# Attention scores of the split pairs: three half-row fp32r passes for two heads at once, in place of two full-row passes for each head

## The chip, the cores and the metric

The kernel runs on one core of a Trainium2 chip. The metric is the device time of one execution in microseconds (us), the median of several runs. A profiled execution gives the trace that the text reads.

## What is computed

Sigmoid attention over 8 batches, 12 heads, 448 rows and 64 columns for a head, and then a bilinear feed-forward network on the 3584 tokens:

```python
scores = scale * np.matmul(q, k.transpose(0, 1, 3, 2)) - np.log(S)
attn = 1.0 / (1.0 + np.exp(-scores))
x = np.matmul(attn, v).transpose(0, 2, 1, 3).reshape(B * S, H * D)
out = (((x @ w1) * (x @ w2)) @ w3) @ w_out
```

Everything is float32. The weights come as 64-bit words that the kernel decodes itself.

## The kernel before

**Pairs and chunks.** Two heads make a pair, since 2 x 64 columns fill 128 partitions; there are 48 pairs. The 448 rows of k are cut into four chunks: three of 128 rows and a short one of 64. For a pair, the kernel goes through the chunks in the order 0, short, 1, 2 (`chunks`); each is one slot of the program. In a slot stand a chunk's scores on TensorE (PE), its sigmoid on ScalarE (ACT), then twelve matmuls of the network's first layer (`take(filler, ups)`, line 361, tile `up`), and then the products with v that are due (`attend`, tile `av`).

**Plain and split pairs.** The first 13 pairs (`PLAIN`) use float32 operands as they are; there, the two heads of a pair stand in the lower and upper 64 partitions, and each head's scores are a matmul over 64 rows (line 200). In the trace such a float32 matmul is two records. The other 35 pairs are split: an operand is written as a rounded high part and the remainder as a low part, both fp32r, whose matmul is one record. The `up` matmuls start with the second slot of the first split pair, so from there on each slot holds work for TensorE that depends on nothing in the slot.

**Scores of a split pair before.** q and k are loaded twice, so that both halves of the partitions hold the same 64 rows. `split_pair` makes `qs` (the high part in the lower 64 partitions, the low part in the upper ones), `kh` and `kl` (high and low part of k in both halves). A matmul of `kh` with `qs` over all 128 rows then sums high and low part of q in one pass, and a second one with `kl` adds the rest: two passes for each head, four for a chunk (line 203). For the short chunk, `ks` holds the high and low parts of its 64 rows of k side by side as 128 columns; one pass for each head (line 229) gives two halves, which `add_halves` (lines 190 and 191) adds with two copies on ACT and two additions on VectorE (DVE). `short_attention` then needs three activations and two subtractions (line 243). A split pair has 3 x 4 + 2 = 14 score passes.

**After the scores.** `attention` runs the sigmoid twice, once into fp32r (`ah`) and once in place (`sp`); DVE subtracts the one from the other (line 221, `al`). The scores stand in PSUM, in two buffers of the tile `sp`. Two more PSUM tiles hold the `av` sums, two the `up` sums.

**Order.** PE and SP (the queue that issues the DMAs) run in the order in which the code is written. For the split pairs, a scheduler sets the order on ACT, DVE and POOL (GpSimd).

The part of the program that this is about, the loop over the pairs, stands at the end of the function printed here.

Of the kernel before, what the change touches and what calls it, by code (L numbers as in the profile page):

```python
# [11 lines left out]
F32 = mybir.dt.float32  # L12
F32R = mybir.dt.float32r
U32 = mybir.dt.uint32
AF = mybir.ActivationFunctionType
ALU = mybir.AluOpType
# [9 lines left out]
def sigmoid_attention_bilinear_ffn(  # L26
# [16 lines left out]
    nc = tc.nc  # L43
    B, H, D, S = qT.shape
    DM, DF = w1.shape[0], w1.shape[1] // 2
    NT = B * S
    P = 128
    CHUNKS = [(c, min(P, S - c)) for c in range(0, S, P)]
    NC = len(CHUNKS)
    assert 2 * D == P and CHUNKS[-1][1] == D  # L50
    NPAIR = H // 2
# [10 lines left out]
    PLAIN = 2 * NPAIR + 1  # L62
# [3 lines left out]
    ps = phase_s.enter_context(tc.tile_pool(name="ps", bufs=3, space=PSUM))  # L66
# [5 lines left out]
    def split(dst_hi, dst_lo, src, hi_engine, lo_engine):  # L72
        hi_engine(out=dst_hi, in_=src)  # L73
        lo_engine.tensor_tensor(out=dst_lo, in0=src, in1=dst_hi, op=ALU.subtract)  # L74
# [40 lines left out]
    pa = phase_a.enter_context(tc.tile_pool(name="pa", bufs=2, side="right"))  # L115
# [10 lines left out]
    def load_pair(b, hp):  # L126

        heads = slice(2 * hp, 2 * hp + 2)
        if b * NPAIR + hp < PLAIN:

            qk = pa.tile([P, 2, S], F32, name="qp", tag="qk", bufs=3)
            for i, src in enumerate((qT, kT)):
                nc.sync.dma_start(out=qk[:, i], in_=src[b, heads].rearrange("h d s -> (h d) s"))
            return qk[:, 0], qk[:, 1]
        qq = pa.tile([P, 2, S], F32, name="qq", tag="qk", bufs=3)
        kk = pa.tile([P, 2, S], F32, name="kk", tag="qk", bufs=3)
        for dst, src in ((qq, qT), (kk, kT)):
            for r in range(2):
                nc.sync.dma_start(
                    out=dst[r * D:(r + 1) * D], in_=src[b, heads].rearrange("h d s -> d h s")  # L140
                )
        return qq, kk

    def load_v(b, hp):
        vv = pa.tile([P, NC, 2 * D], F32, name="vv")
# [6 lines left out]
            nc.sync.dma_start(out=vv[r * D:(r + 1) * D, NC - 1], in_=v[b, full:, cols])  # L152
        return vv

    def split_pair(plain, qq, kk):

        if plain:
            return qq, kk, None, None
        qs = pf[0].tile([P, 2, S], F32R, name="qs")
        kh = pf[0].tile([P, 2, S], F32R, name="kh")  # L160
        kl = pf[0].tile([P, 2, S], F32R, name="kl")
        nc.vector.tensor_copy(out=qs, in_=qq)
        nc.vector.tensor_tensor(out=qs[D:], in0=qq[D:], in1=qs[D:], op=ALU.subtract)
        split(kh, kl, kk, nc.vector.tensor_copy, nc.gpsimd)

        ks = pf[0].tile([P, 2, P], F32R, name="ks")
        for j in range(2):
            for i, k in ((j, kh), (1 - j, kl)):
                nc.gpsimd.tensor_copy(out=ks[:, j, i * D:(i + 1) * D], in_=k[:, j, S - D:])
        return qs, kh, kl, ks  # L170

    def split_v(plain, vv):
        if plain:
            return vv

        vs = pf[0].tile([P, NC, 2, 2, D], F32R, name="vs")
        for j in range(2):
            split(vs[:, :, j, j, :], vs[:, :, j, 1 - j, :], vv[:, :, j * D:(j + 1) * D],
                  nc.vector.tensor_copy, nc.gpsimd)
        return vs  # L180

    def sigmoid(dst, src):
        n = src.shape[0]
        nc.scalar.activation(dst, src, AF.Sigmoid, bias=bias[:n], scale=scale)  # L184

    def add_halves(dst, src):

        for j in range(2):
            rows, others = slice(j * D, (j + 1) * D), slice((1 - j) * D, (2 - j) * D)
            nc.scalar.copy(out=dst[rows], in_=src[j][others])  # L190
            nc.vector.tensor_tensor(out=dst[rows], in0=src[j][rows], in1=dst[rows], op=ALU.add)

    def scores(qs, kh, kl, c):

        at, n = CHUNKS[c]
        sp = ps.tile([P, 2, 512], F32, name="sp", bufs=2)[:n, :, :S]
        for j in range(2):
            if kl is None:
                rows = slice(j * D, (j + 1) * D)
                nc.tensor.matmul(sp[:, j], kh[rows, at:at + n], qs[rows], start=True, stop=True)  # L200
                continue
            for m, k in enumerate((kh, kl)):
                nc.tensor.matmul(sp[:, j], k[:, j, at:at + n], qs[:, j], start=m == 0, stop=m == 1)  # L203
        return sp

    def attention(plain, sp):

        n = sp.shape[0]
        if plain:
            a = pa.tile([P, 2, S], F32, name="ap", tag="ah", bufs=3)[:n]  # L210
            sigmoid(a, sp)
            return (a,)
        ah = pa.tile([P, 2, S], F32R, name="ah", tag="ah", bufs=3)
        sigmoid(ah[:n], sp)
        sigmoid(sp, sp)
        if n < P:

            nc.vector.tensor_tensor(out=ah[n:], in0=sp, in1=ah[:n], op=ALU.subtract)
            return (ah,)
        al = pf[0].tile([P, 2, S], F32R, name="al")  # L220
        nc.vector.tensor_tensor(out=al, in0=sp, in1=ah, op=ALU.subtract)  # L221
        return ah, al

    def short_scores(ks, qs):


        sp = ps.tile([P, 2, 512], F32, name="sp", bufs=2)[:, :, :S]
        for j in range(2):
            nc.tensor.matmul(sp[:, j], ks[:, j], qs[:, j], start=True, stop=True)  # L229
        t = pa.tile([P, S], F32, name="st", tag="t")  # L230
        add_halves(t, [sp[:, j] for j in range(2)])
        return t

    def short_attention(t):

        a = pa.tile([P, 2, S], F32R, name="ah", tag="ah", bufs=3)
        for j in range(2):
            rows = slice(j * D, (j + 1) * D)
            sigmoid(a[rows, j], t[rows])
        sigmoid(t, t)  # L240
        for j in range(2):
            rows, others = slice(j * D, (j + 1) * D), slice((1 - j) * D, (2 - j) * D)
            nc.vector.tensor_tensor(out=a[others, j], in0=t[rows], in1=a[rows, j], op=ALU.subtract)  # L243
        return (a,)

    def attend(c, ops, v, accs):

# [140 lines left out]
    pairs = [(b, hp) for b in range(B) for hp in range(NPAIR)]  # L388
# [11 lines left out]
    qks, vvs = {}, {}  # L400
# [8 lines left out]
    warm = ps.tile([P, 512], F32, name="up", tag="up", bufs=2)  # L409
    for _ in range(16):  # L410
        nc.tensor.matmul(warm[:, :S], zeros[:, :P], zeros, start=True, stop=True)
    splits, vs = {0: split_pair(0 < PLAIN, *qks.pop(0))}, {0: split_v(0 < PLAIN, vvs.pop(0))}
    first = decode_first()
    take(first, 1)
    xs = {n: [] for n in range(NU)}
# [2 lines left out]
    waiting = []  # L418
    accs = {}
    pf = []  # L420
# [14 lines left out]
    def prepare(p, i):  # L435

        n = p + 1
        change = n in (PLAIN, PLAIN + 1)
        if i == (2 if change else 1) and n < len(pairs):
            splits[n] = split_pair(n < PLAIN, *qks.pop(n))  # L440
        if i == 0 and change:
            qks[n] = load_pair(*pairs[n])
        if i == 1 and n < len(pairs):
            vvs[n] = load_v(*pairs[n])
        if i == NC - 1 and n < len(pairs):
            vs[n] = split_v(n < PLAIN, vvs.pop(n))
        n = p + 2
        if i == (0 if n < PLAIN else 2) and n not in (PLAIN, PLAIN + 1) and n < len(pairs):
            qks[n] = load_pair(*pairs[n])

    def x_due(slot):
        for at in [k for k in xts if (k[0] * NPAIR + k[1] + 1) * NC < slot]:
# [9 lines left out]
    chunks = [0, NC - 1, *range(1, NC - 1)]  # L464
    ups = NF * 2 * NK * 3 // PER
    slot = 0
    for p, (b, hp) in enumerate(pairs):
        if p == PLAIN - 1:
            order.close()
            order.enter_context(tc.manual_schedule(engines={ET.PE, ET.SP}))  # L470
        plain = p < PLAIN
        qs, kh, kl, ks = splits.pop(p)
        for i, c in enumerate(chunks):
            if (p, i) == (PLAIN - 1, 2):
                phase_p.close()
                pf.append(phase_a.enter_context(tc.tile_pool(name="pf", bufs=2, side="right")))
            prepare(p, i)
            if not plain and i == 1:
                short = short_scores(ks, qs)
            else:  # L480
                sp = scores(qs, kh, kl, c)
                if not plain and i == 2:
                    waiting.append((slot + 1, p, NC - 1, short_attention(short)))
                waiting.append((slot + 1, p, c, attention(plain, sp)))
            if slot == 0:
                take(first, 10)
            for at, j, stage in steps:
                if at == slot:
                    decode_weights(j, stage)
            x_due(slot)  # L490
            if slot >= BEGIN:
                take(filler, ups)
            attend_due(slot)
            slot += 1
# [25 lines left out]
    for jc in range(NF):  # L520
        take(filler, 10)
        for half in range(2):
            ms = slice(half * NM, (half + 1) * NM)
            src = w_out[jc * P:(jc + 1) * P].rearrange("p (m u) -> p m u", u=2)[:, ms]
# [110 lines left out]
    for i, ic in enumerate(ics):  # L635
        c, second = divmod(i, 2)
# [4 lines left out]
        for half in range(2):  # L641
            ms = slice(half * NM, (half + 1) * NM)
            acc = ps2.tile([P, 512], F32, name="up", tag="acc", bufs=8)
            for jc in range(NF):
                for m, (a, w) in enumerate(((w3h, woh), (w3h, wol), (w3l, woh))):
                    nc.tensor.matmul(  # L646
                        acc[:, :NM], a[:, jc], w[:, jc, ms],
                        start=(jc == 0 and m == 0), stop=(jc == NF - 1 and m == 2),
                    )
            nc.scalar.copy(out=stage[:, 2 * second + half], in_=acc[:, :NM])  # L650
            name = ("b11", None, "b21", "b22")[2 * second + half]
# [109 lines left out]
```

## Time and profile before

| | us |
|---|---|
| median of 3 runs | 1058.15 (1057.02 to 1058.85) |
| the profiled execution, its own time | 1057.37 |
| its span | 1055.5 |
| PE busy | 1042.1 |
| weight loads of PE (PEld) busy | 847.1 |
| DVE busy | 793.8 |
| ACT busy | 592.6 |
| POOL busy | 164.2 |

The stage of the plain pairs lasts to about 110 us, the split pairs to about 700 us, and the layers after them to the end. PE and PEld are one engine: a matmul and the load of its stationary operand, which can run under the matmul before it. A matmul's record holds its passage through the array too, so records overlap; the distance from one start to the next is the time that a pass takes. In a row such as `64*128` after the word MATMUL, the first number is the rows and the second the columns of the array that the matmul uses; `128*128` is the whole array. The chain is the list of work that ended last, followed back from the end.

### The profile page before, as it was taken

How to read it: one execution, taken by the hardware profiler on the slowest of the kernel's cores; microseconds unless marked ns; L12 is line 12 of the kernel's file. 1: busy time of each engine (PE TensorE's matmuls, PEld its weight loads, DVE VectorE, ACT ScalarE, POOL GpSimd, SP SyncE). 2: the span in 40 equal slices, each digit the busy share in tenths (PEclk: the TensorE clock that was granted, in tenths of full speed). 3: DMA queues.
4: the chain of work that ended last, by engine and by line, in shares of the span. 5: the costliest groups of instructions: out<-in, count | busy, mean ns of one | idle time of the engine just before them, and what ended most of it. 6: DMA issues, size and time to landing. Idle time of an engine off the chain costs nothing.

```text
span 1055.5 us, 14196 instructions
## 1 busy us (share of the span) xinstructions
PE 1042.1 (99%) x4820; PEld 847.1 (80%) x4820; DVE 793.8 (75%) x1248; ACT 592.6 (56%) x877; POOL 164.2 (16%) x249
## 2 busy tenths in 40 slices
PE   9998999999999999999999999999999999999998
PEld 3222688888888888888888888878899999999997
DVE  6998788877787787787878777668826677868572
ACT  6887676676667667676666766653324443324230
POOL 0000423222232322223231322100000000000000
PEclk9999999999999999999999999999999999999999
DMA  9886664555546454554555545144324555657542
GB/s 283 261 282 192 157 175 122 164 150 141 137 124 179 133 156 130 142 166 125 137 143 156 154 129 146 41 158 135 115 93 147 181 186 194 223 174 227 174 141 79
DMA packets 118983, 167.56 MB, mean 159 GB/s; under 512 B 10176, under 2 KB 96128, under 8 KB 118912
## 3 DMA queue, kind: packets, MB, share of 16 engines
q1 hardware_dynamic: 118912, 166.67, 52.7%
q8 instruction: 38, 0.62, 0.3%
q14 instruction: 33, 0.27, 0.1%
HBM read 125.73 MB, written 40.89 MB: 158 GB/s over the span
## 4 chain that ended last, share of the span: by engine, by line
PE 91%; DMA 4%; DVE 3%; ACT 1%; issue 1%; SPq 1%; ACTq 0%; DVEq 0%
PE up L361 41%; PE up L679 20%; PE av L259 9%; PE sp L203 8%; PE up L646 5%; PE sp L200 4%; PE av L252 3%; PE sp L229 1%; DMA raw<-w3T 1%; DMA x_dram<-t 1%; DMA vv<-vL 1%; ACT ap L184 1%; DMA graw<-g_dram 0%; DMA qq<-qT 0%; DVE w3l L74 0%
## 5 line engine op out<-in xcount | busy, mean ns | idle before, releaser
L361 PE MATMUL up<-xh,w 128*128 128x512 f32 x1344 | 438.9, 391 | 1.1 <-DVE g L375 1.1
L361 PEld LDWEIGHTS up<-xh,w 128*128 128x128 f32 x1344 | 252.3, 188 | 54.5 <-ACT w3h L73 1.5
L361 PE MATMUL up<-xl,w 128*128 128x512 f32 x672 | 263.1, 392 | 0.0
L184 ACT ACTIVATE ah<-sp,bias 128x896 fp32r<-128x896 f32 x105 | 105.7, 1006 | 112.6 <-PE sp L203 112.5
L221 DVE TENSOR_TENSOR al<-sp,ah 128x896 fp32r<-128x896 f32 x105 | 114.4, 1090 | 63.4 <-ACT sp L184 62.7
L361 PEld LDWEIGHTS up<-xl,w 128*128 128x128 f32 x672 | 126.2, 188 | 23.3
L74 POOL TENSOR_TENSOR kl<-kk,kh 128x896 fp32r<-128x896 f32 x35 | 74.6, 2132 | 403.0 <-DVE kh L73 240.9
L679 PE MATMUL up<-gs,w 128*128 128x448 f32 x576 | 119.3, 367 | 0.0
L679 PEld LDWEIGHTS up<-gs,w 128*128 128x128 f32 x576 | 108.1, 188 | 9.9
L184 ACT ACTIVATE sp<-sp,bias 128x896 f32<-128x896 f32 x105 | 101.9, 970 | 0.0
L259 PE MATMUL av<-ah,vs 128*128 128x448 f32 x280 | 91.9, 369 | 0.0
L679 PE MATMUL up<-ga,w 128*128 128x448 f32 x432 | 89.5, 366 | 0.0
L679 PEld LDWEIGHTS up<-ga,w 128*128 128x128 f32 x432 | 81.1, 188 | 7.1
L259 PE MATMUL av<-al,vs 128*128 128x448 f32 x210 | 77.5, 369 | 0.3 <-DVE al L221 0.3
L203 PE MATMUL sp<-qs,kh 128*128 128x448 f32 x210 | 77.4, 369 | 0.0
L203 PE MATMUL sp<-qs,kl 128*128 128x448 f32 x210 | 77.2, 367 | 0.0
L74 POOL TENSOR_TENSOR vs<-vv,vs 128x256 fp32r<-128x256 f32 x70 | 55.4, 793 | 102.8 <-DVE vs L73 102.8
L73 ACT CAST ga<-graw 128x448 fp32r<-128x448 f32 x48 | 25.8, 566 | 68.6 <-DMA graw<-g_dram 68.6
L243 DVE TENSOR_TENSOR ah<-st,ah 64x448 fp32r<-64x448 f32 x70 | 43.4, 620 | 25.1 <-ACT st L184 23.5
L184 ACT ACTIVATE ap<-sp,bias 128x896 f32<-128x896 f32 (+1 forms) x52 | 52.3, 1006 | 12.5 <-PE sp L200 11.4
L259 PEld LDWEIGHTS av<-ah,vs 128*128 128x128 f32 x280 | 52.6, 188 | 8.3 <-issue 0.2
L252 PE MATMUL av<-ap,vv 128*64 128x448 f32 (+1 forms) x208 | 52.1, 579 | 5.7 <-ACT ap L184 5.3
(73 smaller groups left out, 1504.2 us busy)
## 6 DMA issues: line engine op xcount, KB each, us to landing
graw<-g_dram SPq DMA_DIRECT2D x72, 448.0 KB, 4.3
qq<-qT SPq DMA_DIRECT2D x70, 224.0 KB, 3.7
kk<-kT SPq DMA_DIRECT2D x70, 224.0 KB, 4.4
g_dram<-g SPq DMA_DIRECT2D x56, 256.0 KB, 2.2
raw<-w SPq DMA_DIRECT2D x15, 768.0 KB, 5.9
x_dram<-t SPq DMA_DIRECT2D x48, 224.0 KB, 2.0
xr<-x_dram SPq DMA_DIRECT2D x42, 256.0 KB, 4.3
vv<-vL SPq DMA_DIRECT2D x48, 192.0 KB, 4.1
```

The source lines that it names most:

```text
L73: hi_engine(out=dst_hi, in_=src)
L74: lo_engine.tensor_tensor(out=dst_lo, in0=src, in1=dst_hi, op=ALU.subtract)
L184: nc.scalar.activation(dst, src, AF.Sigmoid, bias=bias[:n], scale=scale)
L200: nc.tensor.matmul(sp[:, j], kh[rows, at:at + n], qs[rows], start=True, stop=True)
L203: nc.tensor.matmul(sp[:, j], k[:, j, at:at + n], qs[:, j], start=m == 0, stop=m == 1)
L221: nc.vector.tensor_tensor(out=al, in0=sp, in1=ah, op=ALU.subtract)
L243: nc.vector.tensor_tensor(out=a[others, j], in0=t[rows], in1=a[rows, j], op=ALU.subtract)
L252: nc.tensor.matmul(accs[0][cols, :S], v[:ops[0].shape[0], c, cols], ops[0][:, j], start=first, stop=last,)
L259: nc.tensor.matmul(accs[j][:, :S], v[:, c, j].rearrange("p u d -> p (u d)"), a[:, j], start=first and m == 0, stop=last and m == len(ops) - 1,
L361: nc.tensor.matmul(acc[:, :TU], w[fc // NH][:, fc % NH, kc], x, start=(kc == 0 and m == 0), stop=(kc == NK - 1 and m == 2),)
L646: nc.tensor.matmul(acc[:, :NM], a[:, jc], w[:, jc, ms], start=(jc == 0 and m == 0), stop=(jc == NF - 1 and m == 2),)
L679: nc.tensor.matmul(acc[:, :TB], w[:, c, ms], g[:, c], start=(c, m) == (0, 0), stop=(c, m) == (NH - 1, 2),)
```

## The change

The scores of a split pair are made as in a plain pair: the two heads stand in the two halves of the partitions. q and k are loaded once, side by side in one tile (`qp`), by two DMAs in place of four; `split` makes one high tile (`qh`) and one low tile (`ql`) of it. A chunk's scores are three passes over 64 rows for each head: high k with high q, high k with low q, low k with high q. The product of the two low parts is left out. The passes of the two heads alternate, in different halves of the array's rows. The short chunk is made in the same way, on 64 columns; `short_scores`, `short_attention` and `ks` are gone, and its low part is one subtraction that was in `attention` already. A split pair has 24 such half passes where it had 14 full ones.

The scores of two chunks are now issued in one go, in the first and in the third slot of a pair (chunks 0 and short, then 1 and 2); the second and fourth slot have none. The products with v are due one or two slots later. `ah` has 4 buffers in place of 3. q and k of a split pair are loaded in the first slot of the pair two before it, as for the plain pairs; before it was the third slot, and for the pairs 13 and 14 the first slot of the pair ahead of them.

```diff
-        qs = pf[0].tile([P, 2, S], F32R, name="qs")
-        kh = pf[0].tile([P, 2, S], F32R, name="kh")
-        kl = pf[0].tile([P, 2, S], F32R, name="kl")
-        nc.vector.tensor_copy(out=qs, in_=qq)
-        nc.vector.tensor_tensor(out=qs[D:], in0=qq[D:], in1=qs[D:], op=ALU.subtract)
-        split(kh, kl, kk, nc.vector.tensor_copy, nc.gpsimd)
...
+        hi = pf[0].tile([P, 2, S], F32R, name="qh")
+        lo = pf[0].tile([P, 2, S], F32R, name="ql")
+        split(hi, lo, qk, nc.vector.tensor_copy, nc.gpsimd)
+        return hi, lo
...
-            for m, k in enumerate((kh, kl)):
-                nc.tensor.matmul(sp[:, j], k[:, j, at:at + n], qs[:, j], start=m == 0, stop=m == 1)
...
+        terms = ((0, 0), (0, 1), (1, 0)) if len(qks) > 1 else ((0, 0),)
+        for m, (kt, qt) in enumerate(terms):
+            for j in range(2):
                 rows = slice(j * D, (j + 1) * D)
+                nc.tensor.matmul(
+                    sp[:, j], qks[kt][rows, 1, at:at + n], qks[qt][rows, 0],
+                    start=m == 0, stop=m == len(terms) - 1,
+                )
...
-        if i == (0 if n < PLAIN else 2) and n not in (PLAIN, PLAIN + 1) and n < len(pairs):
+        if i == 0 and n < len(pairs):
             qks[n] = load_pair(*pairs[n])
...
-            if not plain and i == 1:
-                short = short_scores(ks, qs)
-            else:
-                sp = scores(qs, kh, kl, c)
-                if not plain and i == 2:
-                    waiting.append((slot + 1, p, NC - 1, short_attention(short)))
-                waiting.append((slot + 1, p, c, attention(plain, sp)))
+            if plain:
+                waiting.append((slot + 1, p, c, attention(plain, scores(parts, c))))
+            elif i % 2 == 0:
+                sps = [scores(parts, k) for k in chunks[i:i + 2]]
+                for due, k, sp in zip((2, 2) if i == 0 else (1, 2), chunks[i:i + 2], sps):
+                    waiting.append((slot + due, p, k, attention(plain, sp)))
```

On PE, at the first slot of a split pair in the middle of the attention, this stood before: the last products with v of a slot, the four score passes of chunk 0, and the first of the twelve `up` matmuls.

```order
L259 MATMUL av<-al,vs 128x448
L203 MATMUL sp<-qs,kh 128x448
L203 MATMUL sp<-qs,kl 128x448
L203 MATMUL sp<-qs,kh 128x448
L203 MATMUL sp<-qs,kl 128x448
L361 MATMUL up<-xh,w 128x512
```

At the same place the changed kernel has this (its lines are numbered otherwise: 183 for the scores, 220 for the products with v, 322 for `up`; the name after the arrow that stands first is the moving operand, q, and the second one holds k; where one name stands alone, both are from `qh`):

```order
L220 MATMUL av<-al,vs 128x448
L183 MATMUL sp<-qh 128x448 x2
L183 MATMUL sp<-ql,qh 128x448 x2
L183 MATMUL sp<-qh,ql 128x448 x2
L183 MATMUL sp<-qh 64x448 x2
L183 MATMUL sp<-ql,qh 64x448 x2
L183 MATMUL sp<-qh,ql 64x448 x2
L322 MATMUL up<-xh,w 128x512
```

Four full passes have become six pairs of half passes (x2 stands for the two heads), three of them with 128 columns and three with the 64 of the short chunk, and ahead of them and behind them stand matmuls on the whole array.

On ACT, around the short chunk's slot, this stood before: two copies of the `av` sums, the short chunk's copies and activations, and a chunk's two sigmoids.

```order
L190 COPY t<-av 64x448 x2
L190 COPY st<-sp 64x448 x2
L184 ACTIVATE ah<-st,bias 64x448 x2
L184 ACTIVATE st<-st,bias 128x448
L184 ACTIVATE ah<-sp,bias 128x896
L184 ACTIVATE sp<-sp,bias 128x2x448
L372 COPY a_sb<-up 128x512
```

Now the sigmoids of two chunks stand together, and the short chunk has two activations of 64 partitions among them:

```order
L166 ACTIVATE ah<-sp,bias 128x896
L166 ACTIVATE sp<-sp,bias 128x2x448
L166 ACTIVATE ah<-sp,bias 64x896
L166 ACTIVATE sp<-sp,bias 64x2x448
L172 COPY t<-av 64x448 x2
L333 COPY a_sb<-up 128x512
```

Of the short chunk's five rows two are left, and four activations of two chunks follow each other with nothing between them.

More of the change, by code (lines that the diff above doesn't have):

```diff
@@ L128, in load_pair @@
         heads = slice(2 * hp, 2 * hp + 2)
[L129 to L142, printed above, removed]
+        qk = pa.tile([P, 2, S], F32, name="qp", tag="qk", bufs=3)
+        for i, src in enumerate((qT, kT)):
+            nc.sync.dma_start(out=qk[:, i], in_=src[b, heads].rearrange("h d s -> (h d) s"))
+        return qk
     def load_v(b, hp):
@@ L153, in load_v, with split_pair @@
         return vv
-    def split_pair(plain, qq, kk):
+    def split_pair(plain, qk):
         if plain:
-            return qq, kk, None, None
-        qs = pf[0].tile([P, 2, S], F32R, name="qs")
-        kh = pf[0].tile([P, 2, S], F32R, name="kh")
-        kl = pf[0].tile([P, 2, S], F32R, name="kl")
-        nc.vector.tensor_copy(out=qs, in_=qq)
-        nc.vector.tensor_tensor(out=qs[D:], in0=qq[D:], in1=qs[D:], op=ALU.subtract)
-        split(kh, kl, kk, nc.vector.tensor_copy, nc.gpsimd)
[L166 to L170, printed above, removed]
+            return (qk,)
+        hi = pf[0].tile([P, 2, S], F32R, name="qh")
+        lo = pf[0].tile([P, 2, S], F32R, name="ql")
+        split(hi, lo, qk, nc.vector.tensor_copy, nc.gpsimd)
+        return hi, lo
     def split_v(plain, vv):
@@ L191, in add_halves, with scores @@
             nc.vector.tensor_tensor(out=dst[rows], in0=src[j][rows], in1=dst[rows], op=ALU.add)
-    def scores(qs, kh, kl, c):
+    def scores(qks, c):
         at, n = CHUNKS[c]
         sp = ps.tile([P, 2, 512], F32, name="sp", bufs=2)[:n, :, :S]
-        for j in range(2):
-            if kl is None:
+        terms = ((0, 0), (0, 1), (1, 0)) if len(qks) > 1 else ((0, 0),)
+        for m, (kt, qt) in enumerate(terms):
+            for j in range(2):
                 rows = slice(j * D, (j + 1) * D)
-                nc.tensor.matmul(sp[:, j], kh[rows, at:at + n], qs[rows], start=True, stop=True)
-                continue
-            for m, k in enumerate((kh, kl)):
-                nc.tensor.matmul(sp[:, j], k[:, j, at:at + n], qs[:, j], start=m == 0, stop=m == 1)
+                nc.tensor.matmul(
+                    sp[:, j], qks[kt][rows, 1, at:at + n], qks[qt][rows, 0],
+                    start=m == 0, stop=m == len(terms) - 1,
+                )
         return sp
@@ L209, in attention @@
         if plain:
-            a = pa.tile([P, 2, S], F32, name="ap", tag="ah", bufs=3)[:n]
+            a = pa.tile([P, 2, S], F32, name="ap", tag="ah", bufs=4)[:n]
             sigmoid(a, sp)
             return (a,)
-        ah = pa.tile([P, 2, S], F32R, name="ah", tag="ah", bufs=3)
+        ah = pa.tile([P, 2, S], F32R, name="ah", tag="ah", bufs=4)
         sigmoid(ah[:n], sp)
@@ L222, in attention @@
         return ah, al
[L224 to L244, printed above, removed]
     def attend(c, ops, v, accs):
@@ L411, in sigmoid_attention_bilinear_ffn @@
         nc.tensor.matmul(warm[:, :S], zeros[:, :P], zeros, start=True, stop=True)
-    splits, vs = {0: split_pair(0 < PLAIN, *qks.pop(0))}, {0: split_v(0 < PLAIN, vvs.pop(0))}
+    splits, vs = {0: split_pair(0 < PLAIN, qks.pop(0))}, {0: split_v(0 < PLAIN, vvs.pop(0))}
     first = decode_first()
@@ L437, in prepare @@
         n = p + 1
[L438 to L442, printed above, removed]
+        if i == (2 if n in (PLAIN, PLAIN + 1) else 1) and n < len(pairs):
+            splits[n] = split_pair(n < PLAIN, qks.pop(n))
         if i == 1 and n < len(pairs):
@@ L471, in sigmoid_attention_bilinear_ffn @@
         plain = p < PLAIN
-        qs, kh, kl, ks = splits.pop(p)
+        parts = splits.pop(p)
         for i, c in enumerate(chunks):
```

## The prediction

> **What bounds the kernel now.** I read the page first: busy times of the engines, over the whole span.
>
> ```profile
> PE 1042.1 (99%) x4820; PEld 847.1 (80%) x4820; DVE 793.8 (75%) x1248; ACT 592.6 (56%) x877; POOL 164.2 (16%) x249
> ```
>
> PE is busy for 99%. That average is made of stages, so the view of windows comes next, for 100 us in the middle of the split pairs (columns: length, then busy time and instructions of PE, PEld, DVE, ACT and POOL, the granted clock, DMA).
>
> ```profile
> 200.00:300.00 100.00, 100.00 (x455) 85.10 (x454) 78.94 (x115) 67.07 (x95) 28.14 (x42) 1.00 0.53 145
> ```
>
> Here PE has no idle time at all, at the full clock. DVE, ACT and POOL have 21 to 72% to spare. So whatever the change takes from DVE, ACT, POOL and the DMA queue in this stage is worth nothing by itself: only the time that PE needs for a pair counts, 35 times. The chain of one stretch in order of time (start, length, what) shows what PE does with a pair:
>
> ```profile
> 302.00 0.83 PE sp L203 x4
> 302.83 2.75 PE up L361 x12
> 305.58 0.82 PE sp L203 x4
> 306.40 2.75 PE up L361 x12
> 309.15 1.24 PE av L259 x6
> 310.39 0.83 PE sp L203 x4
> 311.22 2.75 PE up L361 x12
> 313.97 0.83 PE av L259 x4
> 314.79 0.41 PE sp L229 x2
> 315.20 2.75 PE up L361 x12
> ```
>
> A pair's four slots follow each other without a gap. The scores of a pair are three pieces of four passes and one of two: 0.83 + 0.82 + 0.83 + 0.41 = 2.89 us for 14 passes, 0.207 each. That is the part that the change replaces. The products with v and the `up` passes stay in number and size.
>
> **The new passes.** A split pair has 24 half passes now, in 12 couples, one for each head. What a couple takes is the first question. No fp32r half pass is in the trace, but the plain pairs have float32 ones. All of them in a group (total busy, mean ns of one), and one couple from the timeline:
>
> ```profile
> L200 PE MATMUL sp<-qp 64*128 64x448 f32 x156 | 40.9, 602 | 0.0
> ```
>
> ```profile
> 56.22 0.54 PE L200 MATMUL sp<-qp 64*128 64x448 f32 x2
> ```
>
> 156 records of 0.602 us would be 94 us one after another; together they cover 40.9. The couple covers 0.54 us, less than the mean of one record, so the two heads' passes lie on top of each other. I take a couple as one pass. Its length: between the first fp32r passes of the split pairs the starts are 0.20 apart (110.80, 111.00, 111.20 in the fence below), in the chain above 0.207; I take 0.203. Ends: 0.188, the mean of one weight load in the group below, under which I know of no pass; and 2 x 0.108 = 0.216, if the two heads' loads of 0.11 each (worked out below) cannot lie on top of each other.
>
> ```profile
> L361 PEld LDWEIGHTS up<-xh,w 128*128 128x128 f32 x1344 | 252.3, 188 | 54.5 <-ACT w3h L73 1.5
> ```
>
> So the passes fall from 2.89 to 12 x 0.203 = 2.44 us, a gain of 0.45 for a pair, if nothing is lost between half and full passes.
>
> **Switching between the whole array and halves of it.** The diff puts half passes among full ones, which the split pairs did not have. The trace has such places at its start and where the plain pairs end. First the timeline of PE, then that of the weight loads, just ahead of and in the first plain pair:
>
> ```profile
> 6.06 0.36 PE L411 MATMUL up<-zeros 128*128 128x448 f32 x1
> 6.35 0.65 PE L200 MATMUL sp<-qp 64*128 64x448 f32 x2
> ```
>
> ```profile
> 6.35 0.30 PEld L200 LDWEIGHTS sp<-qp 64*128 64x128 f32 x4 [0.30 <-issue]
> 7.30 0.19 PEld L200 LDWEIGHTS sp<-qp 64*64 64x64 f32 x4 [0.65 <-issue]
> ```
>
> ```profile
> 6.83 0.54 PE L200 MATMUL sp<-qp 64*128 64x448 f32 x2
> ```
>
> Then PE where the first split pair follows a plain one:
>
> ```profile
> 110.49 0.47 PE L203 MATMUL sp<-qs,kh 128*128 128x448 f32 x1
> 110.80 0.36 PE L203 MATMUL sp<-qs,kl 128*128 128x448 f32 x1
> 111.00 0.36 PE L203 MATMUL sp<-qs,kh 128*128 128x448 f32 x1
> 111.20 0.37 PE L203 MATMUL sp<-qs,kl 128*128 128x448 f32 x1
> 111.49 0.97 PE L252 MATMUL av<-ap,vv 128*64 128x448 f32 x4
> 112.40 0.68 PE L229 MATMUL sp<-qs,ks 128*128 128x448 f32 x2
> ```
>
> The reader is to see three things. A full pass that has a half pass behind it holds the engine for 0.29 (6.06 to 6.35; 111.20 to 111.49) where 0.20 is usual: 0.09 in which the array empties. The loads for the new mode begin only after that, "issue" being their releaser, so no semaphore held them. Second, the first pass after a switch takes 0.31 (110.49 to 110.80), 0.11 above the usual, which is its own load uncovered. The float32 halves say the same: the first couple takes 0.48 (6.35 to 6.83), the second, whose loads lay under the first, 0.37 and then 0.10 of emptying until 7.30. Third, that 7.30 is a switch between halves of 128 and of 64 columns, so the short chunk's couples have one too; their load of 64 columns is half as long, 0.05. A switch that keeps the columns and changes the rows alone is in the plain pairs, too:
>
> ```profile
> 98.04 0.54 PE L200 MATMUL sp<-qp 64*64 64x448 f32 x2
> 98.51 0.60 PE L252 MATMUL av<-ap,vv 128*64 128x448 f32 x2
> ```
>
> 0.47 from start to start, 0.37 of it the couple's own passage, and 0.10 of emptying again.
>
> One switch in or out: 0.09 + 0.11 = 0.20. One pair has two groups of scores, so two in and two out, 0.80, and one inside the first group, 0.08 + 0.05 = 0.13: together 0.93 us.
>
> **The sum.** 2.44 + 0.93 = 3.37 us for a pair in place of 2.89: +0.48, times 35 pairs +16.8 us. With passes of 0.188 it is 2.26 + 0.93 - 2.89 = +0.30, or +10.5; with 0.216, 2.59 + 0.93 - 2.89 = +0.63, or +22. The issue of two chunks in one go is in this already: with a group for each chunk there would be two switches in and out more.
>
> A rule of the Trainium skill bears on the couples' loads: TensorE: Matmul & The Clock Gate, in Part 3 under The mechanism, says that a weight load overlaps running matmuls only when its row group is another one. By it each couple would wait for its own loads. The trace differs: of the four loads that begin at 6.35, spanning 0.30, the last two begin by 6.35 + 0.30 - 0.19 = 6.46, and the couple they serve begins at 6.83, while the couple in the same two row groups runs. It stays a rival, priced below.
>
> **What else moves, at nothing.** For a pair, DVE loses two operations on `qs`, two on `st` and one subtraction on `ah` net; ACT loses three operations, POOL the four copies to `ks`, SP two DMAs. All of it lies under a PE that is never idle in this stage; a cover that cannot go while PE has 48 `up` passes a pair. One gain may come through: in the attention twelve `up` passes take 2.75, 0.2292 each, and after it
>
> ```profile
> 711.76 65.56 PE up L361 x288
> ```
>
> 0.2276 each. If the lighter engines are why, 1728 passes x 0.0016 gives at most -2.8 us; I take none.
>
> The loads of q and k come two slots earlier, or four for the first two split pairs, and are half the bytes. The tile `qk` has three buffers, and the split of the pair ahead frees one before. Nothing queued behind them on SP comes later by more than two issues.
>
> **New waits.** A group needs both `sp` buffers. They are free when ACT has run four activations and DVE the last subtraction:
>
> ```profile
> L184 ACT ACTIVATE ah<-sp,bias 128x896 fp32r<-128x896 f32 x105 | 105.7, 1006 | 112.6 <-PE sp L203 112.5
> L163 DVE TENSOR_TENSOR qs<-qq,qs 64x896 fp32r<-64x896 f32 x35 | 38.1, 1090 | 1.2
> L372 ACT COPY a_sb<-up 128x512 f32<-128x512 f32 x56 | 33.2, 594 | 15.8 <-PE up L361 11.3 <-ACT st L190 4.4
> ```
>
> At most 4 x 1.01 + 1.09 = 5.1 us after the group (the new subtraction on 64 partitions has the second row's size). Between the first group and the second stand 2.75 + 0.83 + 2.75 = 6.3 us of PE work, between the second and the next pair's first 7.6. Behind the four activations on ACT is queued `a_sb`, for whose `up` bank PE comes back after 18 `up` passes, 4.1 us, and at least one piece of 0.83: 4.9, against 4.0 + 0.6 at the worst. So I cost both at nothing, with up to +3 us as the other end. In the first split pair the two groups are only about 0.97 + 2.75 = 3.7 apart: up to +1.4, once.
>
> Against the profiled execution's own 1057.37 us (its span of 1055.5 and 1.87 around it) the forecast is 1057.37 + 16.8 = 1074.2; the median is 0.78 above that execution, so 1075.0. Ends: 10.5 - 2.8 = +8 and 22 + 3 + 1.4 = +26, so 1066 to 1084.
>
> **The rivals.** *The switches cost nothing for fp32r.* Then 2.44 - 2.89 = -0.45 a pair, -16 us, 1042. It decides where the five switches of a pair cost less than 0.45 together, half of what I took. For it: the half passes in all rows above are float32, and the array might take the next fp32r loads early. Against it: both rows of 0.29 have an fp32r pass ahead, the 0.31 is an fp32r load behind, and nothing in the trace switches for less. Chance 0.09; that it comes out within 0.2%, 0.01.
>
> *The loads of a couple cannot lie under the couple ahead of it.* Nine of the twelve couples (the other three stand right behind a switch, with their load counted) get 0.11 more: +1.0 a pair, +35 us on top, 1110. Against it: 6.46 and 6.83. Chance 0.04.
>
> *fp32r couples do not run side by side.* Twelve more passes, 2.44 a pair, +85 on top, 1160. Against it: the float32 couples. Chance 0.04.
>
> **The numbers.** My own case has 0.82; nearly all of it lies between 1066 and 1084, which is 8 in 10; I give 1065 to 1084. A measurement of this kernel can tell about 0.2%, 2 us, from no change. Faster by more: 0.09; within it: 0.01; slower: 0.82 + 0.04 + 0.04 = 0.90.
>
> **What would show it.** In the changed profile: PE with about 5170 instructions (ten more for each of 35 pairs) and no idle time but at the switches; a chunk's first couple starting 0.29 after the last full pass, a couple each 0.20, the first full pass after a group 0.31; a pair's period 0.48 above the 16.8 that the chain shows now (302.00 to 315.20 and 2.75, and a last piece of 0.83). The `up` passes still 0.229. I am wrong if the loads of the half passes start under a full pass, if couples are further apart than 0.22, or if PE waits for ACT on `sp` or `up` in each pair.

## The result and the profile after

The changed kernel takes 1072.47 us (median of 4 runs, 1070.44 to 1073.70), the kernel before 1057.65 beside it: a ratio of 1.0137, 95% interval 1.0115 to 1.0159. The profiled execution's span is 1069.5 us, 14.0 more than before. Busy times and instructions:

```profile
PE 1053.5 (98%) x5170; PEld 817.8 (76%) x5170; DVE 676.0 (63%) x1073; ACT 549.0 (51%) x772; POOL 127.9 (12%) x109
```

DVE has lost 118 us of work, ACT 44, POOL 36, and PE has gained 350 instructions. The window in the middle of the split pairs shows what that was worth (columns as before: length, PE, PEld, DVE, ACT, POOL, clock, DMA):

```profile
200.00:300.00 100.00, 100.00 (x502) 78.55 (x502) 59.08 (x86) 57.60 (x75) 22.04 (x18) 1.00 0.35 112
```

PE is still at 100 of 100, the lighter engines only stand idle for longer. The chain of a pair in order of time:

```profile
301.01 2.95 PE up L322 x12
303.96 0.82 PE av L220 x4
304.79 2.75 PE up L322 x12
307.53 1.41 PE sp L183 x9
308.94 2.97 PE up L322 x12
311.92 1.24 PE av L220 x6
313.15 2.75 PE up L322 x12
315.90 0.82 PE av L220 x4
316.73 1.41 PE sp L183 x12
```

The nine pieces are one period (the time from one pair to the next), 17.12 us; before it was 16.79 by the same addition. Taken from the starts of the pairs, which are finer, the median period is 16.773 before and 17.127 now, 0.354 more. Twelve `up` passes take 2.75 as before where products with v precede them, and 2.95 or 2.97 behind a group of scores. A group takes 1.41. So the scores cost 2 x 1.41 + 2 x 0.21 = 3.24 us a pair, where the 14 full passes took 2.89. The chain counts 12 or only 9 records for a group, though each has 12: where two lie on top of each other it does not always follow both.

What is in the 1.41 and in the 0.21 shows in the timeline, PE first, then the weight loads:

```profile
316.36 0.37 PE L220 MATMUL av<-al,vs 128*128 128x448 f32 x1
316.66 0.47 PE L183 MATMUL sp<-qh 64*128 64x448 f32 x2
316.97 0.36 PE L183 MATMUL sp<-ql,qh 64*128 64x448 f32 x2
317.17 0.37 PE L183 MATMUL sp<-qh,ql 64*128 64x448 f32 x2
317.37 0.36 PE L183 MATMUL sp<-qh 64*64 64x448 f32 x2
317.57 0.36 PE L183 MATMUL sp<-ql,qh 64*64 64x448 f32 x2
317.77 0.37 PE L183 MATMUL sp<-qh,ql 64*64 64x448 f32 x2
318.07 0.50 PE L322 MATMUL up<-xh,w 128*128 128x512 f32 x1
318.40 0.39 PE L322 MATMUL up<-xl,w 128*128 128x512 f32 x1
```

```profile
316.65 0.18 PEld L183 LDWEIGHTS sp<-qh 64*128 64x128 f32 x2 [0.31 <-issue]
316.76 0.19 PEld L183 LDWEIGHTS sp<-ql,qh 64*128 64x128 f32 x2
316.97 0.19 PEld L183 LDWEIGHTS sp<-qh,ql 64*128 64x128 f32 x2
317.17 0.14 PEld L183 LDWEIGHTS sp<-qh 64*64 64x64 f32 x2
...
318.07 0.19 PEld L322 LDWEIGHTS up<-xh,w 128*128 128x128 f32 x1 [0.36 <-issue]
```

The last full pass holds the engine for 0.30 (316.36 to 316.66), the loads begin after it, the first couple takes 0.31, and the following ones 0.20 each, both halves within 0.36 to 0.37 us. The last couple holds the engine for 0.30 (317.77 to 318.07), and the first full pass takes 0.33 where an `up` pass takes 0.23. Between 317.17 and 317.37, where the couples go from 128 to 64 columns, the distance is 0.20: there is no switch to be seen.

One wait of PE is new. The view of waits from 110 to 740 us:

```profile
PE sp L183 <- DVE al L204: 1.8, 1, 1.8
PE up L322 <- DVE g L336: 1.1, 1, 1.1
PE sp L183 <- DVE ah L201: 0.3, 1, 0.3
```

The first and the third, 1.76 and 0.25 in the timeline, are in the first split pair, where the second group waits for the `sp` buffers. The second stood before too, with the same 1.1.

### The profile page after: what moved, and what is told of

Same layout as the page of the kernel before. It is cut to its first block, busy times and chain, and to the rows that moved or that the text cites. A ratio compares the mean times of both kernels' runs of the same rounds, so it can differ in the third digit from the quotient of the medians.

```text
span 1069.5 us, 14278 instructions
## 1 busy us (share of the span) xinstructions
PE 1053.5 (98%) x5170; PEld 817.8 (76%) x5170; DVE 676.0 (63%) x1073; ACT 549.0 (51%) x772; POOL 127.9 (12%) x109
## 4 chain that ended last, share of the span: by engine, by line
PE 85%; DVE 2%; DMA 1%; ACT 0%; issue 0%; DVEq 0%; ACTq 0%; SPq 0%
PE up L322 43%; PE up L634 19%; PE av L220 9%; PE sp L183 9%; PE up L601 5%; DMA graw<-g_dram 0%; DVE w3l L74 0%; DMA w3l<-w_dram 0%; DMA raw<-w_out 0%; DVE graw L513 0%; ACT w3h L73 0%; DVE g L336 0%; DVE f L98 0%; ACT gs L73 0%; DVE raw L103 0%
## 5 line engine op out<-in xcount | busy, mean ns | idle before, releaser
L322 PE MATMUL up<-xh,w 128*128 128x512 f32 x1344 | 447.4, 397 | 1.1 <-DVE g L336 1.1
L166 ACT ACTIVATE ah<-sp,bias 128x896 fp32r<-128x896 f32 (+1 forms) x140 | 140.9, 1006 | 194.2 <-PE sp L183 194.2
L166 ACT ACTIVATE sp<-sp,bias 128x896 f32<-128x896 f32 (+1 forms) x140 | 136.1, 972 | 0.0
L220 PE MATMUL av<-ah,vs 128*128 128x448 f32 x280 | 97.5, 368 | 0.0
L74 POOL TENSOR_TENSOR ql<-qp,qh 128x896 fp32r<-128x896 f32 x35 | 74.4, 2125 | 176.4 <-DMA qp<-kT 107.0
L183 PE MATMUL sp<-qh 64*128 64x448 f32 (+1 forms) x280 | 58.6, 415 | 2.0 <-DVE al L204 1.8
L74 DVE TENSOR_TENSOR xl<-xr,xh 128x512 fp32r<-128x512 f32 x42 | 31.3, 745 | 44.5 <-ACT xh L73 44.5
L336 DVE TENSOR_TENSOR g<-up,a_sb 128x512 f32<-128x512 f32 x56 | 38.6, 689 | 30.8 <-PE up L322 30.2
```

The lines of the kernel that those rows point to most:

```text
L183: nc.tensor.matmul(sp[:, j], qks[kt][rows, 1, at:at + n], qks[qt][rows, 0], start=m == 0, stop=m == len(terms) - 1,)
L220: nc.tensor.matmul(accs[j][:, :S], v[:, c, j].rearrange("p u d -> p (u d)"), a[:, j], start=first and m == 0, stop=last and m == len(ops) - 1,
L322: nc.tensor.matmul(acc[:, :TU], w[fc // NH][:, fc % NH, kc], x, start=(kc == 0 and m == 0), stop=(kc == NK - 1 and m == 2),)
L336: nc.vector.tensor_tensor(out=g, in0=acc, in1=a_sb, op=ALU.mult)
```

## The experiments

**Each chunk by itself.** In the changed kernel, the groups of two are taken apart:

```diff
-            if plain:
-                waiting.append((slot + 1, p, c, attention(plain, scores(parts, c))))
-            elif i % 2 == 0:
...
+            waiting.append((slot + 1, p, c, attention(plain, scores(parts, c))))
```

> The changed kernel, but each chunk's scores in a slot of their own, so a split pair has four groups of half passes instead of two; passes, loads and splits as changed. Theory (a move between full and half passes costs about 0.20 us, 0.40 for a group in and out): two more groups, +0.8 us a pair, the period from 17.13 to about 17.9, and the wait of the first split pair gone (-2): +26 us, about 1098. Rival one (the loss comes from issuing two chunks in one go, by bursts on ScalarE or the score buffers): the period falls toward the 16.78 of before. Rival two (the half passes themselves are slow): the period stays at 17.13.

Measured: 1096.72 us, a ratio to before of 1.0355 (1.0338 to 1.0372). The chain of some slots:

```profile
308.26 2.94 PE up L322 x12
311.20 0.83 PE av L220 x4
312.02 0.76 PE sp L183 x6
312.79 2.95 PE up L322 x12
315.74 0.82 PE av L220 x4
316.56 0.82 PE sp L183 x6
```

Every `up` piece is now 2.94 or 2.95, and the starts of the pairs are 17.87 apart, 0.74 more than with two groups. The passes are the same, so a group costs 0.37 by being one. Both rivals fall: issuing two chunks in one go is what spares time here. The wait for `sp` in the first split pair is gone, as expected, but not all of its time: PE waits there 1.1 for `al` instead.

**The chunks in another order.**

```diff
-    chunks = [0, NC - 1, *range(1, NC - 1)]
+    chunks = [0, 1, NC - 1, 2]
```

> The changed kernel with the chunks in the order 0, 1, short, 2: the groups are (0, 1) and (short, 2), so the columns change from 64 to 128 inside a group, and in the very first plain pair two float32 couples of the same 64*128 form follow each other. If a change of columns costs fp32r couples nothing either way: period 17.13 again, 1072 within 3. If only the change from 128 to 64 is free: +0.13 a pair, period 17.26, +4.5. In the plain pair: if the 0.10 of emptying is a switch, the second 64*128 couple follows the first with its loads under it, 0.37 after its last pass starts; if it belongs to every float32 couple, the loads start 0.47 after it as before.

Measured: 1071.67 us, 1.0124 (1.0100 to 1.0147), and a period of 17.07. The group that begins with the short chunk:

```profile
325.73 0.39 PE L322 MATMUL up<-xh,w 128*128 128x512 f32 x1
326.04 0.42 PE L183 MATMUL sp<-qh 64*64 64x448 f32 x2
326.30 0.37 PE L183 MATMUL sp<-ql,qh 64*64 64x448 f32 x2
326.50 0.37 PE L183 MATMUL sp<-qh,ql 64*64 64x448 f32 x2
326.70 0.37 PE L183 MATMUL sp<-qh 64*128 64x448 f32 x2
```

From 64 to 128 columns (326.50 to 326.70) is as free as the other way. The first couple after the switch takes 0.26 in place of 0.31, since its load has 64 columns; that is the 0.05 by which the period is shorter. And in the first plain pair, where two float32 couples of the form 64*128 follow each other, the loads of the second chunk begin at 7.93 and 8.30, each under a pass that starts there:

```profile
7.44 0.30 PEld L183 LDWEIGHTS sp<-qp 64*128 64x128 f32 x4 [0.30 <-issue]
7.93 0.19 PEld L183 LDWEIGHTS sp<-qp 64*128 64x128 f32 x2 [0.18 <-issue]
8.30 0.19 PEld L183 LDWEIGHTS sp<-qp 64*128 64x128 f32 x2 [0.18 <-issue]
```

The two chunks' loads are 0.86 apart (7.44 to 8.30), where a change from 128 to 64 columns made it 0.95 in the kernel before (6.35 to 7.30). So a float32 couple does not empty the array as such; the change of form does.

**One head after the other.**

```diff
-        for m, (kt, qt) in enumerate(terms):
-            for j in range(2):
+        for j in range(2):
+            for m, (kt, qt) in enumerate(terms):
```

> The changed kernel with the loops over heads and terms exchanged: three half passes of one head, then three of the other. Theory (PE takes passes in program order, and only neighbours in different halves lie on top of each other): per chunk the third pass of the first head can share with the first of the second, 5 pass times instead of 3, so 8 x 0.203 = 1.62 us more a pair, period 18.75, +57 us, about 1129. Rival (each half has a queue of its own, and the order does not matter): period 17.13, 1072.

Measured: 1071.89 us in one run, period 17.12. My theory falls. The trace shows the couples as if nothing had been exchanged:

```profile
316.34 0.48 PE L183 MATMUL sp<-qh 64*128 64x448 f32 x2
316.65 0.37 PE L183 MATMUL sp<-ql,qh 64*128 64x448 f32 x2
316.85 0.38 PE L183 MATMUL sp<-qh,ql 64*128 64x448 f32 x2
```

Two passes of the same term start together, although the program has the three terms of one head first. Either the two halves go through their passes each by itself, or the order was exchanged on the way to the chip; the trace has the starts of the passes and not the order in which they were issued.

**Groups of two with full rows.** The operands and passes of before, with the groups and the short chunk of the changed kernel (`t` has one buffer, for room):

```diff
-            for j in range(2):
+        for j in range(2):
...
+            for m, k in enumerate(qks[1:]):
+                nc.tensor.matmul(
+                    sp[:, j], k[:, j, at:at + n], qks[0][:, j], start=m == 0, stop=m == 1
+                )
```

> The changed kernel's groups of two chunks and its short chunk, but with q and k loaded and split as before and two passes over all 128 rows for each head: no half rows, 16 full passes a pair, four of them with 64 columns. Theory (grouping costs nothing but the wait of the first split pair, and only a change of rows drains the array): 16 x 0.207 = 3.31 against 2.90 before, period 16.78 + 0.41 = 17.19, 1058 + 14.5 + 2 = 1074. If changing columns alone drains the array among full passes too: 0.3 to 0.4 a pair more, period about 17.55, 1086. Rival (two chunks in one go cost by themselves): the period is above 17.19 with idle time of PE in each pair.

Measured: 1072.99 us, 1.0136 (1.0121 to 1.0151), period 17.18, against 17.19 expected. PE at the short chunk:

```profile
317.21 0.37 PE L200 MATMUL sp<-qs,kl 128*128 128x448 f32 x1
317.41 0.36 PE L200 MATMUL sp<-qs,kh 128*64 128x448 f32 x1
...
318.02 0.36 PE L200 MATMUL sp<-qs,kl 128*64 128x448 f32 x1
318.22 0.40 PE L338 MATMUL up<-xh,w 128*128 128x512 f32 x1
```

All steps are 0.20, in and out of 128*64: of the changes tried with fp32r, only that of rows costs. It also settles that the 0.20 at a group's edges is no wait for its buffers: the groups stand here as in the changed kernel, and no step shows it. Without half passes, groups of two cost nothing in the steady pairs but the two added passes.

**The `up` passes one slot earlier.** In the changed kernel:

```diff
-    BEGIN = 2 * PER + NC + 1
+    BEGIN = 2 * PER + NC
```

> The changed kernel with the up matmuls beginning one slot earlier, in the first slot of the first split pair, so that 2.75 us more of PE work stands between that pair's two groups of scores. Theory (PE waits there 1.76 and 0.25 us because the second group needs score buffers that VectorE still reads): the wait falls to under 0.3, the rest stays, -1.9 us against the changed kernel, about 1070.5. Rival (the stretch is late for another reason, such as operands that are not split yet): the wait stays or moves and the time does too.

Measured: 1072.63 us, 1.0131 (1.0117 to 1.0144), which cannot be told from the changed kernel. The wait for `sp` is gone, as expected, and this is the only wait of PE left between 110 and 740 us:

```profile
PE up L322 <- DVE g L336: 2.7, 1, 2.7
```

It was 1.1. It stands at 723 us, where the attention is over and DVE works on the next weights ahead of `g`. In this execution that gives back 1.6 of the 2.0 us saved, and more than the rest goes right behind it: by the view of windows the clock granted to TensorE is 0.50 from 727.0 to 730.4, where the changed kernel has 1.00 at that place, and half of 3.4 is 1.7 us. So the theory of the wait holds, but the forecast of the time, 1070.5, does not.

**Both kernels again.** Two more traces, unchanged, for the plain pairs, which the change issues alike.

> The kernel before, once more, for its trace. In the first one the first split pair begins at 110.49 us, in the changed kernel at 111.50, and the plain pairs ahead of it are issued alike. If that 1.0 us is the run's own variation, this run begins elsewhere within about 1 us; if the change makes it, 110.5 again.

> The changed kernel once more, for the same question: the start of the first split pair varies within about 1 us around 111 if it is the run's own variation, and is 111.5 again if the change makes it. The period stays at 17.13.

Measured: 1058.27 and 1074.31 us in one run each. The first split pair starts at 110.66 in the kernel before, at 112.48 in the changed one. In the changed kernel's first trace and the five experiments above it starts between 111.25 and 112.34. So it comes later in the changed kernels, by 0.6 to 2.0 us.

In the second trace of the changed kernel the first period is also longer, 18.27 in place of 16.77, with 17.13 for all the later ones as before: PE waits 2.2 in one piece, and behind that the granted clock is 0.50 from 120.1 to 123.5 us, so that twelve `up` passes take 3.38. The run with the other order of chunks has the same (a wait of 2.3, a clock of 0.50 from 119.8 to 123.2, a first period of 18.32).

Of the 0.6 to 2.0 us, by the starts of the plain pairs, a part is there from the first pair on (6.3 us before, 6.3 to 7.6 after). That part may be the runs' own variation: the kernel of the next experiment has the start of the kernel before and is at 6.75. The rest, 0.1 to 0.8 us, comes in most of them in the stretch from 73 to 97 us, in which ACT waits some 5 us for a load of weights in both kernels and the granted clock is 0.50 for 6.8 us in all, in both too. The kernel with full rows has the loads of before and is late too, so the loads are not the cause, or not alone. What is stays open: the plain pairs' matmuls are issued alike, but their sigmoids have four buffers in place of three (`ap` shares those of `ah`), and no run took that edit and the others apart.

**Grouping where there are switches already.** The kernel before, with the plain pairs alone changed: scores of two chunks in one go, products of two chunks in one go, in the order 0, 1, 2, short.

```diff
...
+            if plain and i % 2 == 0:
+                sps = [scores(qs, kh, kl, k) for k in (i, i + 1)]
+                for k, sp in zip((i, i + 1), sps):
+                    waiting.append((slot + 2, p, k, attention(plain, sp)))
...
```

> The kernel before, with its split pairs untouched, but in the plain pairs the scores of two chunks in one go and the products of two chunks in one go, in the order 0, 1, 2, short. Couples of one form then follow each other, which empties nothing, so a plain pair has 6 switches where it had 8: up to 2 x 0.2 x 13 = 5 us if PE alone bounds the plain stage. VectorE is busy for over 80% of that stage and ScalarE waits 5.3 us for a load in it, so I expect the first split pair 0 to 4 us earlier than 110.5 and the total between 1054 and 1058. Rival (the stage hangs on VectorE and loads altogether): no change. Each change of a float32 couple from 128 to 64 columns should show the 0.09 of emptying that was seen once, if it is a rule for float32.

Measured: 1055.74 us, 0.9972 (0.9963 to 0.9981): faster than both. A plain pair takes 7.01 us where it took 7.36, 0.35 for two switches fewer, and the first split pair starts at 106.96, 3.5 earlier. That is within the 0 to 4 us expected, and the rival falls. Not all of the 3.5 need be the grouping: in the stretch from 76 us on, the granted clock is 0.50 for 3.4 us here and for 6.8 in the kernel before. The 0.35 is read before 70 us, where the clock is full in both. The weight loads of two groups:

```profile
44.45 0.30 PEld L200 LDWEIGHTS sp<-qp 64*128 64x128 f32 x4 [0.70 <-ACT ap L184]
45.41 0.19 PEld L200 LDWEIGHTS sp<-qp 64*64 64x64 f32 x4 [0.65 <-ACT t L267]
46.31 0.20 PEld L252 LDWEIGHTS av<-ap,vv 128*64 128x64 f32 x4 [0.71 <-issue]
46.74 0.14 PEld L252 LDWEIGHTS av<-ap,vv 128*64 128x64 f32 x2 [0.23 <-issue]
47.11 0.14 PEld L252 LDWEIGHTS av<-ap,vv 128*64 128x64 f32 x2 [0.23 <-issue]
```

Products of one form follow each other 0.37 to 0.43 apart (46.31, 46.74, 47.11), with the loads under the passes. From 64*128 to 64*64, float32 couples still take 0.96 (44.45 to 45.41), as alone: for float32 that change empties the array each time, where for fp32r it is free. (The releasers named there, ACT, do not set this: the rows at 6.35 and 7.30 us before name none and are as far apart.)

## Why the prediction was right, and where its sum was off

The forecast was +16.8 us, the median moved by 14.8 and the span by 14.0.

**The couples**, forecast at 0.203 with 0.54 us of evidence from float32 alone, are 0.20 apart. The rivals in which they run one after another, or wait for their own loads, are out: the loads of 316.97 lie under the couple that starts there in the same halves. The Trainium skill says in TensorE: Matmul & The Clock Gate, Part 3, The mechanism, that a load overlaps running matmuls only where the row group differs; the trace does not agree. The same section of the Trainium skill also lets a load run ahead into the background weight buffer, and by that sentence the couples' loads are no surprise; which buffer a load goes to, no trace here tells.

**A switch in or out**, forecast at 0.20, costs just that. In the experiment with each chunk by itself, two groups more were 0.74 a pair, and one of them, the short chunk's, has the 0.05 shorter first load, so (0.74 + 0.05) / 4 = 0.20. The rival of free switches fails on that.

**The term that was mis-sized** is the switch inside the first group, from 128 to 64 columns: forecast at 0.13 a pair, measured at nothing. It was taken from the row at 7.30 us, a float32 couple, as if the type did not matter; for fp32r it does, in both directions and with full rows too. That is 0.13 x 35 = 4.6 us too much, and it is all of the difference between the forecast period (+0.48) and the measured one (17.127 - 16.773 = +0.35).

**Waits that I costed at nothing.** In the steady pairs there are none, as forecast. In the first split pair I had nothing, with up to 1.4 us as the other end; the trace has 2.0. The plain stage, which I had put at nothing, is 1.0 longer. By the starts of the split pairs the 14.0 us of the span are these: 1.0 ahead of the first split pair, 2.1 in it (14.67 before, 16.77 now), 11.1 in the 33 periods after it, and -0.2 from the start of the last one on. The 11.1 are a little under 33 x 0.35 = 11.7, since the second period before was 17.33, 0.6 above its others. The wait in the first split pair is shown by its rows; the cause of the plain stage's part is not known.

**Luck.** That the forecast is only 2.0 above the median, or 2.8 above the span, is in part luck: one term was 4.6 too high, and the other way about 3 us were there that I had put at nothing.

**The relief of DVE, ACT, POOL and DMA** was worth nothing, as forecast, and the 2.8 us that I left as an end did not come through either: `up` passes between full ones still take 2.75 for twelve, with DVE at 59 in place of 79 of 100.

## What to carry to other kernels

Count passes of the array and also its changes of form: where TensorE is the bound, a saving of two passes in fourteen was lost nearly twice over to four changes of rows, 0.20 us each. Passes over part of the rows want long groups. An estimate from these numbers: a chunk of 128 rows saves one pass of four, 0.2 us, and a group costs two changes of rows, 0.40, so a group gains only from a third such chunk on; no run here had one. What other engines are spared counts for nothing while TensorE is never idle. A kernel that changes form already can gain by grouping the same forms: the total fell by 3 us here.

## What the runs showed of the hardware that was not expected

- The order of the two heads' passes in the program did not matter: with three passes of one head ahead of three of the other, the heads' passes still start in couples, and the period is 17.12 against 17.13. The trace does not say at which step between program and array this comes about.
- A change of columns with the rows kept (64*128 and 64*64, 128*128 and 128*64) costs fp32r passes nothing, 0.20 from start to start; between float32 couples, 64*128 to 64*64 empties the array in each of the traces read for it, 0.10 us and the load.
- The granted clock fell to 0.50 for 3.4 us behind three waits of PE after the plain pairs (2.2 us in the changed kernel's second trace, 2.3 with the other order of chunks, 2.7 with the `up` passes one slot earlier) and cost 1.7 us each time; behind the 1.8 us of the changed kernel's first trace it stayed at 1.00. Executions of one kernel differ in this, and a wait can so cost more than its own length. What decides it, no run here shows.
